# Three weight loads of an expert stage wait for the rows of group 1 instead of the candidates' rows

## The chip, the core and the metric

The kernel runs on one core of a Trainium2 chip. The metric is the device time of one execution in microseconds, as the median of several runs; the profile shows one execution of the same program, and its span is a little shorter than that execution's time. The engines are named as in the profile: PE (matmul), DVE (vector), ACT (scalar), POOL, and SP, which here only issues transfers.

## What is computed

Attention in chunks of 64 keys gives a matrix x of 4608 rows and 512 columns. A gate picks one of 8 experts for each row; each expert keeps at most 80 rows, those with the highest gate weight, and runs a two-layer network on them. All other rows of the output are zero.

```python
expert_idx = np.argmax(x @ w_gate, axis=1)
...
for e in range(E):
    tok_idx = np.where(expert_idx == e)[0]
    ...                                    # at most `capacity` of them, by gate weight
    h = np.maximum(x[tok_idx] @ w1[e], 0.0)
    out[tok_idx] = gate_w[tok_idx, None] * (h @ w2[e])
```

Here w1 of one expert is 512 x 1024 and w2 is 1024 x 512, both in 32-bit floats, 2 MB each.

## The kernel before

Attention, gate and choice of rows fill the first 132 us or so; x is written to a scratch tensor `xs` in DRAM on the way. The expert stage follows, and only it matters here.

**Rows and groups.** Each of the 8 experts has 96 slots, three quarters of 32. Six groups r = 0 to 5 of 128 slots, four quarters each, are worked off one after the other. Quarter g of group r belongs to expert (4r + g) // 3, so group 0 needs experts 0 and 1, group 1 experts 1 and 2, group 2 experts 2 and 3, group 3 experts 4 and 5, group 4 experts 5 and 6, group 5 experts 6 and 7. The rows of group 0 come another way: two gathers `xc[0]` and `xc[1]` (lines 876 to 878) fetch the candidates' rows of experts 0 and 1 while the ranking still runs, and a matmul (line 920) sorts them into `xT0`. The rows of groups 1 to 5 are gathered by POOL with an indirect transfer each (`gather`, line 181; `rows`, line 170) into the tiles `xg[r]`, 128 rows of 2 KB, once their row numbers `gic` are there (line 151).

**Order on PE.** For each group: first layer, first half of its columns (`layer1(r, 0)`, line 207); transposes of the group before (`hpose`, line 225); transposes of the next group's rows (`xpose`, line 193); first layer, second half; second layer of the group before (`layer2`, line 241). Group 1's transposes stand in the middle of `layer1(0, 1)` (lines 203 and 204): 48 of group 0's 64 first-layer matmuls lie ahead of them.

**Order on SP.** One queue issues all large transfers, in the order of the program. The weights of experts 0 and 1 and w1 of expert 2 (line 968) are loaded before the expert stage. `ahead(r, ...)` (line 960) issues what list r of `LATER` names: pair (e, 0) is w1 of expert e, (e, 1) its w2, (e, 2) a clear, which writes 1 MB of zeros to block e of the output.

```python
LATER = [[(2, 1), (3, 0), (3, 1)], [(4, 0), (5, 0), (0, 2)], [(4, 1), (5, 1), (1, 2)], [(6, 0), (6, 1), (2, 2), (7, 0)], [(7, 1), (3, 2), (4, 2), (5, 2), (6, 2), (7, 2), (8, 2)], [], [], []]
```

List 0 is issued before group 0's first layer, list r + 1 after group r. Where `part` (line 950) is given a column `after`, DVE first copies that column into the weight tile (line 957), and the load, which overwrites it, has to wait for the copy; this holds the load back until `after` is there. Only the three loads of list 0 have such a copy: in the kernel before, the w2 of expert 2 is tied to `xc[0]`, both loads of expert 3 to `xc[1]`. The weight tiles of experts 5, 6 and 7 reuse buffers of earlier experts and so also wait for PE.

**The end.** POOL scatters each group's result into the output (line 260), and no scatter may start before all nine clears have landed.

Of the kernel before, what the change touches and what calls it, by code (L numbers as in the profile page):

```python
# [54 lines left out]
def attention_moe(ctx: ExitStack, tc: tile.TileContext, qk, vv, wg, w1, w2, cap, cst, out):  # L55
# [50 lines left out]
    weights = {}  # L106
# [34 lines left out]
    def place(pool, pp, pt, sel, cb, tag, r0=0, r1=NR):  # L141

        pl = (pp([P, r1 - r0, 5]) if pt is None else
              pp.tile([P, r1 - r0, 5], F32, name=f"pl{tag}{r0}", tag=pt))
        for g in range(4 * r0, 4 * r1):
            o = 32 * (g % 4)
            nc.tensor.matmul(pl[o:o + 32, g // 4 - r0, :], lhsT=sel(*divmod(g, 3)),
                             rhs=cb[:, :, g // 3], start=True, stop=True, tile_position=(0, o))
        gi = pool.tile([P, r1 - r0], I32, name=f"gi{tag}{r0}", tag=f"gi{r0}")
        with nc.allow_low_precision(reason="row numbers are whole and far below 2^24"):  # L150
            nc.vector.tensor_reduce(gi, pl[:, :, 0:2], axis=AX.X, op=ALU.add)
        return pl, gi

    def targets(pool, places, tag):

        gate = pool.tile([P, NR], F32, name=f"gate{tag}", tag="gate")
        row = pool.tile([P, NR], F32, name=f"row{tag}", tag="row")
        r0 = 0
        for pl, gi in places:
            cols = slice(r0, r0 + gi.shape[1])  # L160
            r0 = cols.stop
            nc.vector.tensor_reduce(gate[:, cols], pl[:, :, 2:5], axis=AX.X, op=ALU.add)
            nc.vector.tensor_reduce(row[:, cols], pl[:, :, 0:2], axis=AX.X, op=ALU.add)
        sv = pool.tile([P, NR], F32, name=f"sv{tag}", tag="sv")
        nc.vector.scalar_tensor_tensor(
            sv, gate, 0.0, ct[:, C_OOB:C_OOB + NR], op0=ALU.is_equal, op1=ALU.mult)
        nc.vector.tensor_tensor(sv, sv, row, op=ALU.add)
        return gate, sv
# [5 lines left out]
            in_offset=bass.IndirectOffsetOnAxis(ap=at, axis=0),  # L174
            bounds_check=NT * 512 - 1, oob_is_err=False)

    def experts(pool, pp, gi, si, gate, getw, tag, extra=None, xc=None, xT0=None):
        groups = [[(4 * r + g) // 3 for g in range(4)] for r in range(NR)]
        xg, xT, hs, hT = {}, {}, {}, {}

# [5 lines left out]
        def xpose(r):  # L186
            t = pool.tile([P, 4, P], F32, name=f"xt{tag}{r}", tag="xt")
            n = 4 if r else 2
            for b0 in range(0, 4, n):
                pm = pp.tile([P, n, P], F32, name=f"xp{tag}{r}_{b0}", tag="hp" if b0 else "xp",  # L190
                             bufs=2 if b0 else 1)
                for b in range(n):
                    nc.tensor.transpose(pm[:, b, :], xg[r][:, P * (b0 + b):P * (b0 + b + 1)],  # L193
                                        ident)
                nc.scalar.copy(t[:, b0:b0 + n], pm)
            xT[r] = t
# [69 lines left out]
        for r in range(1, NR) if extra else range(2):  # L266
            gather(r)
        if extra:
            extra(0, xc)
            xT[0] = xT0  # L270
            y0 = pp.tile([P, DM], F32, name=f"y{tag}0", tag="y", bufs=1)
        else:
            xpose(0)
# [17 lines left out]
    with ExitStack() as actx:  # L291
# [371 lines left out]
        def clear(n, eng=nc.sync):  # L663

            r0 = 512 * n
            eng.dma_start(
                out[r0:r0 + 4 * P].rearrange("(p c) d -> p c d", p=P),
                zero[:, None, :].to_broadcast([P, 4, DM]))
# [16 lines left out]
        with tc.manual_schedule():  # L685
# [190 lines left out]
            xc = [mp.tile([P, DM], F32, name=f"xc{e}") for e in range(2)]  # L876
# [39 lines left out]
            xT0 = mp.tile([P, 4, P], F32, name="xT0")  # L916
# [18 lines left out]
            pl, gi = place(mp, bank, None, sel_part, cb, "c")  # L935
            gate, sv = targets(mp, [(pl, gi)], "c")
            nc.vector.tensor_tensor(sv, sv, slot_oob, op=ALU.add)
            si = mp.tile([P, NR], I32, name="si")
# [5 lines left out]
    with tc.manual_schedule():  # L944
        with ExitStack() as ectx:
            ep = ectx.enter_context(tc.tile_pool(name="exp", bufs=2, reuse_waits="tile"))
            pp = ectx.enter_context(tc.tile_pool(name="pexp", bufs=2, space=PSUM,
                                                 reuse_waits="tile"))

            def part(e, l, after=None):  # L950

                w = weights.setdefault(e, [None, None])
                pool = wp if e in (5, 6) else wp2
                a, src, n = ((4, w1, FF), (8, w2, DM))[l]
                w[l] = pool.tile([P, a, n], F32, name=f"w{l + 1}_{e}", tag=f"w{l + 1}")
                if after is not None:
                    nc.vector.tensor_copy(w[l][:, 0, 0:1], after)
                nc.sync.dma_start(w[l], src[e].rearrange("(c p) f -> p c f", p=P))

            def ahead(r, xg):  # L960

                for e, l in LATER[r]:
                    if l < 2:
                        part(e, l, xg[e - 2][:, 0:1] if r == 0 else None)
                    else:
                        clear(e, nc.sync)

            part(2, 0)
            experts(ep, pp, lambda r: gi[:, r:r + 1], si, gate, weights.get, "c", ahead, xc, xT0)


    with tc.If(nc.values_load(flag_i[0:1, 0:1], min_val=0, max_val=1) > 0):  # L972
        with ExitStack() as gctx:
# [59 lines left out]
            with tc.For_i(0, nc.values_load(nr[0:1, 0:1], min_val=0, max_val=48), 1):  # L1033
                with ExitStack() as lctx:
                    xp = lctx.enter_context(tc.tile_pool(name="gx", bufs=1))
                    si = xp.tile([P, NR], I32, name="gsi")
                    with ExitStack() as pctx:
                        lp = pctx.enter_context(tc.tile_pool(name="gpc2", bufs=1, space=PSUM))
                        cand, cb = compact(xp, lp, ptok, "g")
                        pl = place(xp, lp, "pl", lambda e, j: id_b[:, 32 * j:32 * j + 32], cb, "g")  # L1040
                        gate, sv = targets(xp, [pl], "g")
                        nc.vector.tensor_copy(si, sv)
                        nc.vector.tensor_scalar(ptok, ptok, -float(SL), None, op0=ALU.add)
                    with ExitStack() as pctx:
                        lp = pctx.enter_context(tc.tile_pool(name="gpe", bufs=2, space=PSUM))
                        ep = pctx.enter_context(tc.tile_pool(name="gex", bufs=1))
                        gw = {}

                        def getw2(e):
                            if e not in gw:  # L1050
                                gw[e] = load_w(wp2, e, "g")
                            return gw[e]
                        experts(ep, lp, lambda r: pl[1][:, r:r + 1], si, gate, getw2, "g")
# [67 lines left out]
```

## Time and profile before

| | |
|---|---|
| median of 3 runs | 238.54 us (238.28 to 240.3) |
| the profiled execution | 238.45 us |
| its span | 236.6 us |
| PE busy | 219.5 us, 93% of the span |
| DMA queue of SP | 81.31 MB |
| gathers and scatters (POOL's queue) | 3.15 MB |
| weight loads of 2 MB each | 12, median 16.8 us from issue to landing |

A busy PE is not a PE at its peak. "Landing" counts from the start of the issue, and behind other transfers in the queue it is mostly waiting. PEclk is the granted clock of PE, 1.00 for 2.4 GHz and 0.50 for 1.2 GHz.

### The profile page before, as it was taken

What the parts mean: (1) busy time and instruction counts of PE and PEld (TensorE: products, weight loads), DVE (VectorE), ACT (ScalarE), POOL (GpSimd) and SP (SyncE); (2) the same over time, 40 slices, a digit from 0 to 9 for tenths busy, and PEclk for the clock granted to TensorE, in tenths of its full rate; (3) what the DMA queues carried; (4) which work ended last, traced back from release to release, by engine and by line L of the source; (5) the groups of instructions that cost most, each with busy time, mean ns of one, the idle gap of its engine ahead of it and who ended that gap; (6) DMA issues with size and microseconds to landing.
All of it is one profiled execution on the core that took longest, in us unless ns stands there. A gap on an engine that the chain in (4) does not pass through costs nothing.

```text
span 236.6 us, 7355 instructions
## 1 busy us (share of the span) xinstructions
PE 219.5 (93%) x3195; PEld 141.0 (60%) x3195; DVE 115.7 (49%) x249; ACT 67.0 (28%) x119; POOL 57.9 (24%) x158
## 2 busy tenths in 40 slices
PE   8789999999999999989889959999999999999960
PEld 5689889898988888878668412424334343233210
DVE  7858677878787868787686501202111112111110
ACT  2214433545454545454632110202002011010000
POOL 9300401222222222228785440000000000000641
PEclk9999999999999999999999997999999999999997
DMA  6999999999999999999996499999999999999231
GB/s 253 398 413 377 395 406 409 408 408 409 408 410 400 390 399 343 339 372 407 404 414 229 125 386 407 389 409 414 399 408 417 409 415 397 404 405 352 84 115 40
DMA packets 34822, 84.99 MB, mean 359 GB/s; under 512 B 3040, under 2 KB 3168, under 8 KB 34784
## 3 DMA queue, kind: packets, MB, share of 16 engines
q1 hardware_dynamic: 33744, 81.31, 89.2%
q0 software_dynamic: 1040, 3.15, 3.6%
q8 instruction: 27, 0.44, 0.7%
q14 instruction: 11, 0.09, 0.1%
HBM read 64.27 MB, written 20.45 MB: 358 GB/s over the span
## 4 chain that ended last, share of the span: by engine, by line
PE 81%; DMA 8%; DVE 3%; issue 3%; SPq 1%; POOL 1%; ACT 1%; POOLq 0%; ACTq 0%
PE yc L241 17%; PE hc L207 16%; PE o L428 15%; PE s L371 13%; PE px L400 5%; PE pt L400 4%; DMA qb<-in_qk 3%; PE small L480 3%; DMA xgc<-xs,gic 3%; PE hpc L225 3%; DMA xc<-xs,gi_c 1%; PE xpc L193 1%; PE two L862 1%; PE small L491 1%; PE small L603 1%
## 5 line engine op out<-in xcount | busy, mean ns | idle before, releaser
L241 PE MATMUL yc<-w,htc 128*32 128x512 f32 x384 | 42.3, 592 | 0.0
L207 PE MATMUL hc<-w,xtc 128*32 128x512 f32 x320 | 37.2, 606 | 0.0
L428 PE MATMUL o<-vb,pT 128*64 128x130 f32 x576 | 36.1, 276 | 0.7 <-ACT pT L409 0.7
L371 PE MATMUL s<-qb 128*64 128x128 f32 x512 | 31.5, 276 | 2.1 <-DMA qb<-in_qk 1.7
L428 PEld LDWEIGHTS o<-vb,pT 128*64 128x64 f32 x576 | 31.6, 135 | 1.9 <-ACT pT L409 0.8
L371 PEld LDWEIGHTS s<-qb 128*64 128x64 f32 x512 | 27.7, 137 | 4.3 <-issue 2.8
L241 PEld LDWEIGHTS yc<-w,htc 128*32 128x32 f32 x384 | 12.4, 110 | 28.3 <-issue 28.3
L382 DVE TENSOR_REDUCE mx<-s 128x16 f32<-128x1024 f32 x18 | 22.0, 1225 | 13.5 <-PE s L371 12.8
L409 ACT ACTIVATE pT<-pt 128x1024 f32<-128x1024 f32 x18 | 18.3, 1024 | 30.3 <-PE pt L400 30.3
L260 POOL DMA_INDIRECT out<-ysc,to x6 | 5.9, 990 | 85.3 <-SPq L972 81.3
L207 PEld LDWEIGHTS hc<-w,xtc 128*32 128x32 f32 x320 | 10.2, 113 | 23.1 <-issue 23.1
L471 ACT COPY xT<-px 128x1024 f32<-128x1024 f32 x17 | 17.1, 1007 | 22.0 <-PE px L400 22.0
L443 DVE TENSOR_TENSOR x<-o,rc 128x1024 f32<-128x1024 f32 (+1 forms) x20 | 22.4, 1118 | 0.7
L387 DVE TENSOR_TENSOR sm<-s,mx 128x1024 f32<-128x1024 f32 x18 | 22.1, 1227 | 0.6
L212 ACT ACTIVATE hsc<-hc 128x512 f32<-128x512 f32 x6 | 3.6, 597 | 63.5 <-PE hc L207 63.5
L246 DVE TENSOR_SCALAR ysc<-yc,gatec 128x512 f32<-128x512 f32 x6 | 4.5, 751 | 33.5 <-PE yc L241 33.5
L214 DVE TENSOR_SCALAR hsc<-hc 128x512 f32<-128x512 f32 x6 | 4.2, 692 | 26.7 <-PE hc L207 26.7
L229 DVE COPY htc<-hpc 128x512 f32<-128x512 f32 x6 | 4.2, 692 | 22.9 <-PE hpc L225 22.9
L581 ACT ACTIVATE lv<-io_b,bo 128x256 bf16<-128x256 bf16 x29 | 12.5, 499 | 0.8 <-DVE bo L561 0.6
L400 PE MATMUL pt<-ct,sm 64*128 64x64 f32 x288 | 12.6, 228 | 0.0
L400 PE MATMUL px<-ct,x 64*128 64x64 f32 x272 | 12.2, 229 | 0.0
L400 PEld LDWEIGHTS pt<-ct,sm 64*128 64x128 f32 x288 | 10.3, 139 | 2.9 <-issue 2.8
(147 smaller groups left out, 226.6 us busy)
## 6 DMA issues: line engine op xcount, KB each, us to landing
w<-in_w SPq DMA_DIRECT2D x12, 2048.0 KB, 16.8
qb<-in_qk SPq DMA_DIRECT2D x32, 512.0 KB, 7.9
vb<-in_vv SPq DMA_DIRECT2D x36, 260.0 KB, 7.0
out<-zero SPq DMA_DIRECT2D x9, 1024.0 KB, 16.0
xs<-x SPq DMA_DIRECT2D x16, 512.0 KB, 7.6
w<-in_w SPq DMA_DIRECT2D x16, 512.0 KB, 8.0
w<-in_qk SPq DMA_DIRECT2D x4, 512.0 KB, 5.3
xs<-x SPq DMA_DIRECT2D x4, 256.0 KB, 8.3
```

The costliest lines, as they stand in the source:

```text
L207: nc.tensor.matmul(h[o:o + 32, :], lhsT=xT[r][:, b, o:o + 32], rhs=getw(groups[r][g])[0][:, b, 512 * f:512 * f + 512], start=(b == 0), sto ...
L225: nc.tensor.transpose(pm[:, j, :], hs[r][:, P * c:P * c + P], ident)
L241: nc.tensor.matmul(y[o:o + 32, :], lhsT=hT[r][c // 4][:, c % 4, o:o + 32], rhs=getw(groups[r][g])[1][:, c, :], start=(c == 0), stop=(c == ...
L371: nc.tensor.matmul(ps[64 * u:64 * u + 64, t, P * pr:P * pr + P].rearrange("p (h k) -> p h k", h=2), lhsT=t8[:, 1, pr, u, :], rhs=t8[:, 0:3 ...
L382: nc.vector.tensor_reduce(d['mx'], d['s8'], axis=AX.X, op=ALU.max)
L387: nc.vector.tensor_tensor(d['sm'].rearrange("p c k h -> p h c k"), d['s8'], d['mx'][:, :, :, None].to_broadcast([P, 2, 8, 64]), op=ALU.sub ...
L400: nc.tensor.transpose(at[:, 64 * c:64 * c + 64], src(c)[rows], ident[rows, rows])
L409: nc.scalar.activation(d['pT'], pt, AF.Exp, scale=0.125)
L428: nc.tensor.matmul(po[64 * u:64 * u + 64, o:o + 130].rearrange("p (h x) -> p h x", h=2), lhsT=d['pT'][:, u, c:c + 64], rhs=v[:, :, pr, u, ...
L443: nc.vector.tensor_tensor(TT[T][:, r:r + nt, :].rearrange("p r (k h e) -> p (r k) h e", k=4, h=2), pov[..., 0:64], rc[:, :, :, None].to_br ...
L471: nc.scalar.copy(XT[n].rearrange("p c u j -> p u c j"), pm.rearrange("p u (c j) -> p u c j", j=64))
L581: nc.scalar.activation(lv, io_b, AF.Sign, bias=bo[:, rt:rt + 1], scale=-1.0)
```

## The change

The column that the three loads of list 0 wait for is now `xg[1]`, the rows of group 1, for all three. Since `xg` is what `ahead` gets anyway after each group, the parameter `xc` of `experts` goes.

```diff
-    def experts(pool, pp, gi, si, gate, getw, tag, extra=None, xc=None, xT0=None):
+    def experts(pool, pp, gi, si, gate, getw, tag, extra=None, xT0=None):
...
         if extra:
-            extra(0, xc)
+            extra(0, xg)
             xT[0] = xT0
...
                 for e, l in LATER[r]:
                     if l < 2:
-                        part(e, l, xg[e - 2][:, 0:1] if r == 0 else None)
+                        part(e, l, xg[1][:, 0:1] if r == 0 else None)
...
-            experts(ep, pp, lambda r: gi[:, r:r + 1], si, gate, weights.get, "c", ahead, xc, xT0)
+            experts(ep, pp, lambda r: gi[:, r:r + 1], si, gate, weights.get, "c", ahead, xT0)
```

## Rows read from the trace of the kernel before

**Rows 1.** The page's head: the span.
```profile
span 236.6 us, 7355 instructions
```

**Rows 2.** The chain that ended last: start us, us, what.
```profile
127.49 3.33 DMA xc<-xs,gi_c
...
132.78 7.52 DMA xgc<-xs,gic
...
141.00 6.98 PE hc L207 x48
...
149.01 0.44 PE xpc L193 x4
149.45 3.57 PE hc L207 x32
...
159.89 3.43 PE hc L207 x32
...
190.55 3.43 PE hc L207 x32
...
205.88 3.43 PE hc L207 x32
```

**Rows 3.** Stretches: length, busy of PE, PEld, DVE, ACT, POOL; clock, DMA share, GB/s.
```profile
128.00:129.00 1.00, 1.00 (x12) 0.88 (x10) 0.93 (x6) 0.00 (x0) 0.49 (x1) 1.00 0.75 258
142.00:143.00 1.00, 1.00 (x10) 0.22 (x4) 0.00 (x0) 0.00 (x0) 0.00 (x0) 0.50 1.03 397
...
131.80:136.00 4.20, 4.00 (x62) 1.47 (x65) 1.59 (x11) 0.65 (x2) 2.61 (x3) 1.00 0.58 167
136.00:140.00 4.00, 1.82 (x20) 0.32 (x12) 0.00 (x0) 0.60 (x1) 2.57 (x4) 1.00 1.02 385
140.00:145.00 5.00, 4.65 (x28) 1.54 (x32) 0.69 (x1) 0.58 (x1) 0.00 (x0) 0.68 1.04 399
145.00:217.00 72.00, 72.00 (x660) 24.93 (x652) 9.93 (x14) 8.19 (x14) 0.00 (x0) 1.00 1.04 406
```

**Rows 4.** Timeline (start, duration us; idle before); and line 172's five gathers (duration ns).
```profile
131.67 0.56 DVE L957 COPY w<-xc 128x1 f32<-128x1 f32 x3
...
131.89 16.81 SPq L958 DMA_DIRECT2D w<-in_w  x5
...
140.35 0.66 PE L193 MATMUL xpc<-ct,xgc 128*128 128x128 f32 x4 [2.52 <-DMA xgc<-xs,gic]
...
L172 POOL DMA_INDIRECT xgc<-xs,gic x5: 994/998/999, 132.8 to 138.0; - x5
```

**Rows 5.** Issue (ns, start us) and landing (us): w1 of experts 3, 6, 7, last clear.
```profile
L958 SPq DMA_DIRECT2D w<-in_w x1: 524/524/524, 132.4 to 132.4; - x1
...
DMA to landing us min/median/max: 17.3/17.3/17.3
...
L958 SPq DMA_DIRECT2D w<-in_w x1: 2551/2551/2551, 170.0 to 170.0; - x1
...
DMA to landing us min/median/max: 16.0/16.0/16.0
...
L958 SPq DMA_DIRECT2D w<-in_w x1: 2589/2589/2589, 182.6 to 182.6; - x1
...
DMA to landing us min/median/max: 16.2/16.2/16.2
...
L666 SPq DMA_DIRECT2D out<-zero x1: 2603/2603/2603, 206.4 to 206.4; - x1
...
DMA to landing us min/median/max: 13.1/13.1/13.1
```

**Rows 6.** Timeline of POOL at the end: first, fifth and sixth scatter.
```profile
220.48 1.04 POOL L260 DMA_INDIRECT out<-ysc,to  x1 [81.29 <-SPq L972]
...
226.36 0.98 POOL L260 DMA_INDIRECT out<-ysc,to  x1 [0.28 <-issue]
...
230.39 0.98 POOL L260 DMA_INDIRECT out<-ysc,to  x1 [2.86 <-DVE ysc L246]
```

## The prediction

> **What bounds the kernel now.** I read the chain that ended last first. From 141 us on its links are matmuls of the expert stage without a gap, up to the last scatter; ahead of them stands one long transfer, the gather of group 1's rows, 7.52 us from issue to landing, while a gather of the same size on the same line, `xc[1]`, took 3.33 [rows 2]. Group 1's transposes start at 140.35 after 2.52 us in which PE had nothing to do [rows 4], so PE ran dry at 137.83; soon after it works at a granted clock of 0.50, which is 1.2 GHz, as the stretch from 142 to 143 shows [rows 3]. So the chain holds a stall and its echo.
>
> Second I read the stretches, because the chain shows only who ended last. The DMA engines carry 406 GB/s from 145 to 217 us at a share of 1.04 [rows 3]: the transfers are as full as PE. Over that time one queue, in one order, moves weights and clears, and whatever delays its start by D delays every landing by D. The reader should see two lines that run side by side to the end: PE, and SP's stream of transfers.
>
> Third I read where the second line touches the first. Two points matter. The w1 of expert 6 is issued at 170.05 and lands 16.0 us later, at 186.05 [rows 5]; group 4's first layer wants it at 190.55 [rows 2], 4.5 us later. And the last clear, issued at 206.4, lands at 219.5 [rows 5]; the first scatter starts at 220.48 after a wait that the row puts on SP, not on PE [rows 6]. Scatters one to five start at 220.48 to 226.36, 1.47 us apart, so the sixth could start at 227.83; it starts at 230.39, when its data are there [rows 6]. POOL thus has 2.56 us to spare against PE.
>
> **What the change does.** No instruction is added or taken away. Three copies on DVE, 0.56 us together, and the three loads behind them wait for another tile [rows 4]. A copy now follows gather 1, so it moves past the row numbers (line 151) on DVE's queue; behind it on DVE nothing is needed before group 0's ReLU, whose matmuls are not finished at that time, so the wait costs nothing on DVE. If that cover were gone, what waits is the ReLU of group 0 and with it `hpose(0)`. On SP it is different: the w2 of expert 2 is at the head of the queue, and all other loads and clears stand behind it. That delay is the price.
>
> *Gain on PE.* In the kernel before, gather 1 shares the engines with the loads, which SP issues at 131.89, 0.9 us ahead of it [rows 2, 4]. Now it runs alone. I take 3.33 us from `xc[1]` [rows 2]: landing at 132.78 + 3.33 = 136.11, ahead of 137.83. The bounds are 3.33 and the 7.52 of the crowded one; I take the lower, since gather 1 would have as little beside it as `xc[1]` had. The stall of 2.52 goes. With it goes the slow clock: the transposes took 0.66 where the next ones took 0.44, and 48 matmuls took 6.98 where 32 take 3.57, so 48 take 5.36 [rows 2, 4]. That is 0.22 + 1.62. Gain: 2.52 + 0.22 + 1.62 = 4.4 us, at group 1.
>
> *Loss on the stream.* A landing at 140.30 let PE start at 140.35 [rows 2, 4], and from the first copy's start to the first load's issue it is 131.89 - 131.67 = 0.22 us [rows 4]. So SP issues at 136.11 + 0.05 + 0.22 = 136.4, 4.5 us later than before. The stream doesn't lose all of that, since the gathers, 5 x 0.262 = 1.31 MB, used to run amid the loads and now run partly ahead of them. I count bytes up to 140.5, which is 4.5 us past the end of the loads' slow start at 136. Before (1 GB/s is 1 KB per us): 4.2 x 167 + 4 x 385 + 0.5 x 399 = 2440 KB [rows 3]. After: the same slow start of the loads, 4.2 x 167 = 700 KB, now from 136.3 to 140.5, and gather 1, 262 KB, ahead of it. What the other gathers move during the slow start is the open price. Least: nothing, 960 KB in all, D = (2440 - 960) / 406 = 3.6 us. Most: their own pace, one per 1.3 us [rows 4], 3.2 of them, 850 KB, 1810 in all, D = 1.55. Between them I take what the engines have free: the slow start leaves 1.04 - 0.58 of a share for 4.2 us, 1.93, and gathers alone move 258 KB per 0.75 of a share [rows 3], so 660 KB, 1620 in all, D = 820 / 406 = 2.0 us. Should gather 1 take some 0.4 us longer, D grows by about 0.3.
>
> The rows speak of a trade that isn't even: from 131.8 to 136 the share is 0.58 [rows 3], so a load that comes late leaves engines idle. The Trainium skill, "DMA: Bandwidth & Descriptors", section "Issuing engines are not separate DMA queues", says that transfers of all engines run on the same 16 DMA engines and interleave; by that alone the stream would lose what gather 1 gains, and the sum would be 236.5 instead of 237.9.
>
> *The sum.* With D = 2.0, the w1 of expert 6 lands at 188.05, while PE, 4.4 us ahead, wants it at 186.15. A new wait of 1.9 us arises, and PE's lead shrinks to 2.5. The w1 of expert 3 (landing at 132.4 + 17.3 = 149.7, wanted at 159.89) and that of expert 7 (198.8, wanted at 205.88) have 10.2 and 7.1 us [rows 2, 5], less PE's lead of 4.4 and 2.5, against a delay of 2.0: no wait. If PE's clock falls again after the new wait, as it did after the 2.52 us, that costs up to 1.84 more, and the lead is 0.66. The clears end 2.0 later, too: the first scatter at 222.5, the sixth ready at 227.83 + 2.0 = 229.8, against 230.39 before. So the last scatter moves by max(-2.5, 2.0 - 2.56) = -0.56 us, and with the slower clock by the same -0.56. Nearly half of the 4.4 us goes into the wait for expert 6's weights, and most of the rest into the wait for the clears, which set the end. On the profiled execution, 238.45 us (its span of 236.6 [rows 1] and 1.85 around it), this gives 237.9. That execution is 0.1 below the median shown, which I don't correct for.
>
> **The rivals.**
>
> *The stream loses next to nothing.* If engines made up at once for the late start, the loads would lose only gather 1's bytes, 0.262 MB at 406 GB/s, D = 0.65: the scatters move by 0.65 - 2.56 = -1.9, to 236.5. The rule of the Trainium skill quoted above comes to the same. Even at D = 0 POOL's spare of 2.56 bounds the gain: 235.9. Against it: the slow start itself, a share of 0.58 for 4.2 us [rows 3], for which I see no reason to vanish.
>
> *The scatters start without the clears.* Then PE's lead of 2.5 us alone counts: 235.95, faster by just over 1%. Against it: the row of the first scatter waits on SP's side, and it starts 0.98 us after the last clear's landing [rows 5, 6].
>
> *The gather is no faster alone* (the other side). If the 7.52 us are POOL's five issues in a row (132.8 to 138.0 [rows 4]) and not the loads beside them, gather 1 lands at 140.3 as before, PE keeps stall and slow clock, and SP issues at 140.57, 8.7 us late. Bytes up to 144.7: before 4.2 x 167 + 4 x 385 + 4.7 x 399 = 4115 KB; after, 1310 of gathers and 700 of the slow start; D = 2105 / 406 = 5.2. The scatters move by 5.2 - 2.56 = +2.6: 241.1, slower by 1.1%. It decides from D = 4.95 on. Against it: `xc[1]`, too, was one of a pair of gathers, and took 3.33.
>
> *The loads get no credit for the gathers* (D = 3.6 to 4.5). The end moves by +1.0 to +1.9: 239.5 to 240.4, within 1%. With D = 3.6 and a second slow clock, PE loses 3.5 + 1.84 of its 4.4 and comes to +0.9, no later than POOL.
>
> **How the numbers follow.** A measurement of this kernel can tell about 1% from no change, 2.4 us. The forecast with D from 1.2 to 3.6, 237.1 to 239.5, gets 0.65; no credit, to 240.4, gets 0.15; the stream that loses next to nothing 0.07, a quarter of it at 236.05 or less; scatters without the clears 0.03; the slow gather 0.1, all of it slower by over 1%. That is faster 0.05, same 0.85, slower 0.1. The range takes in the forecast, nearly all of the case without credit and the upper end of the faster ones: 236.9 to 240.3.
>
> **What would show it.** Right: gather 1 lands 3.3 to 3.8 us after its issue; no idle time of PE ahead of group 1's transposes; clock 1.00 through 145 us; SP's loads issued from about 136.4; a new idle time of PE of 1.5 to 2.5 us, put on a weight load, ahead of group 4's first layer; the last clear landing 2 us later; six scatters back to back, 1.47 us apart, none waiting for its data. Wrong: a landing of gather 1 after 138; the last clear within 0.5 us of its old place (then the stream lost nothing); a wait for weights at another group; the sixth scatter still waiting for data, which would put PE, not the clears, last.

## The result: slower by 0.7%

| | before | after |
|---|---|---|
| median, 20 runs each | 238.63 us | 240.14 us |
| profiled execution | 238.45 us | 239.59 us |
| its span | 236.6 us | 237.8 us |

The ratio after to before is 1.0071, with a 95% interval of 1.0042 to 1.010. The time lies in the range that the prediction gave, but on the other side of before: a gain of 0.55 us was forecast (238.45 to 237.9), and a loss of 1.1 (profiled executions) to 1.7 us (ratio) was measured.

Four views of the changed kernel answer to rows of before. First the timeline at the start of the expert stage (start, duration, engine and line, and in brackets the idle time before, with what ended it), which answers to [rows 4]:

```profile
132.83 1.00 POOL L172 DMA_INDIRECT xgc<-xs,gic  x1 [4.37 <-DVE rowc L163]
136.28 0.43 DVE L957 COPY w<-xgc 128x1 f32<-128x1 f32 x3 [2.47 <-DMA xgc<-xs,gic]
136.49 1.00 SPq L958 DMA_DIRECT2D w<-in_w  x2
...
137.80 0.66 PE L193 MATMUL xpc<-ct,xgc 128*128 128x128 f32 x4
```

Gather 1 is there when DVE's copies start, at 136.28; SP issues its first load at 136.49, and PE goes into group 1's transposes with no idle time at all. Then the stretches (columns as in [rows 3]):

```profile
131.80:136.30 4.50, 4.29 (x63) 1.56 (x66) 1.33 (x9) 0.65 (x2) 2.86 (x3) 1.00 0.31 80
136.30:140.50 4.20, 4.20 (x40) 1.35 (x36) 0.34 (x3) 1.18 (x2) 2.33 (x4) 1.00 0.80 211
140.50:145.00 4.50, 4.50 (x44) 2.07 (x36) 0.82 (x2) 1.14 (x2) 0.00 (x0) 1.00 1.00 374
...
190.00:191.00 1.00, 1.00 (x8) 0.20 (x4) 0.00 (x0) 0.00 (x0) 0.00 (x0) 0.50 1.04 406
```

The clock is 1.00 at group 1 now, and 0.50 at 190. Up to 145 the engines have moved 360 + 886 + 1683 = 2930 KB since 131.8; in the kernel before it was 700 + 1540 + 1995 = 4235 KB [rows 3]. Third, issue and landing of gather 1, of gather 4, of expert 6's w1 and of the last clear, which answer to [rows 5] (ns of the issue, its start in us; below, us to landing):

```profile
L172 POOL DMA_INDIRECT xgc<-xs,gic x1: 997/997/997, 132.8 to 132.8; - x1
...
DMA to landing us min/median/max: 3.4/3.4/3.4
...
L172 POOL DMA_INDIRECT xgc<-xs,gic x1: 999/999/999, 136.7 to 136.7; - x1
...
DMA to landing us min/median/max: 8.2/8.2/8.2
...
L958 SPq DMA_DIRECT2D w<-in_w x1: 2511/2511/2511, 173.4 to 173.4; - x1
...
DMA to landing us min/median/max: 16.2/16.2/16.2
...
L666 SPq DMA_DIRECT2D out<-zero x1: 2602/2602/2602, 209.9 to 209.9; - x1
...
DMA to landing us min/median/max: 13.0/13.0/13.0
```

Expert 6's w1 lands at 189.6 instead of 186.05, the last clear at 222.9 instead of 219.5. Fourth, the timeline ahead of group 4 and at the end, which answers to [rows 6]:

```profile
186.12 1.03 PE L207 MATMUL hc<-w,xtc 128*32 128x512 f32 x4
...
189.64 1.92 PE L207 MATMUL hc<-w,xtc 128*32 128x512 f32 x5 [2.49 <-DMA w<-in_w]
...
224.04 1.04 POOL L260 DMA_INDIRECT out<-ysc,to  x1 [84.80 <-DVE ysc L246]
...
229.64 0.75 DVE L246 TENSOR_SCALAR ysc<-yc,gatec 128x512 f32<-128x512 f32 x1 [6.12 <-PE yc L241]
229.92 0.98 POOL L260 DMA_INDIRECT out<-ysc,to  x1 [0.28 <-POOL to L259]
231.37 0.98 POOL L260 DMA_INDIRECT out<-ysc,to  x1 [0.28 <-POOL to L259]
```

The kernel before in the same view, at group 4 and at the last result:

```profile
190.37 2.33 PE L207 MATMUL hc<-w,xtc 128*32 128x512 f32 x20
...
228.87 0.75 DVE L246 TENSOR_SCALAR ysc<-yc,gatec 128x512 f32<-128x512 f32 x1 [6.12 <-PE yc L241]
```

Counted from the issue of gather 1 (132.78 before, 132.83 now), PE reaches group 4 4.3 us ahead of before, at 53.29 instead of 57.59. It does four matmuls of expert 5, stands still for 2.49 us until expert 6's weights are there, and then works at the slow clock. This spends more than the lead: the last result starts at 96.81, 0.72 us later than the 96.09 of before. The scatters run back to back, and the sixth has no wait for its data any more, but only just: before, it started 1.52 us behind the start of that result, which now makes 231.16, and its turn comes at 231.37. (The bracket at 224.04 names DVE, but DVE's result of that time was ready at 223.52 and belongs to the fifth scatter; the clear landed at 222.9. A wait for several things is put down to the one that came last.)

Executions differ by up to 2.3 us in when the expert stage begins (gather 1 is issued at 132.61 in e2, at 134.93 in e1), so below I count from the issue of gather 1: the first scatter comes 87.70 us after it in the kernel before (220.48 - 132.78) and 91.21 in the changed one, the last 97.61 and 98.54. The first figure less 87.70 is D, the delay of SP's stream, in the runs that leave no clear out and move none.

### The profile page after: what moved, and what is told of

Its sections match the earlier page's. It is cut to its first block, busy times and chain, and to the rows that moved or that the text cites. A ratio compares the mean times of both kernels' runs of the same rounds, so it can differ in the third digit from the quotient of the medians.

```text
span 237.8 us, 7354 instructions
## 1 busy us (share of the span) xinstructions
PE 219.9 (92%) x3195; PEld 140.6 (59%) x3195; DVE 115.6 (49%) x249; ACT 67.0 (28%) x119; POOL 58.0 (24%) x158
## 4 chain that ended last, share of the span: by engine, by line
PE 73%; DMA 12%; SPq 7%; DVE 3%; issue 1%; POOL 1%; ACT 1%; POOLq 0%; ACTq 0%
PE o L428 15%; PE hc L207 14%; PE s L371 13%; PE yc L241 12%; DMA w<-in_w 7%; PE px L400 5%; PE pt L400 4%; SPq L666 4%; DMA qb<-in_qk 3%; PE small L480 3%; PE hpc L225 2%; DMA xc<-xs,gi_c 2%; SPq L958 1%; PE pwarm L920 1%; PE two L862 1%
## 5 line engine op out<-in xcount | busy, mean ns | idle before, releaser
L207 PE MATMUL hc<-w,xtc 128*32 128x512 f32 x320 | 38.8, 614 | 2.5 <-DMA w<-in_w 2.5
```

Of the source, the lines that this page charges most:

```text
L207: nc.tensor.matmul(h[o:o + 32, :], lhsT=xT[r][:, b, o:o + 32], rhs=getw(groups[r][g])[0][:, b, 512 * f:512 * f + 512], start=(b == 0), sto ...
```

## The experiments

Three theories. **Clears**: D holds back the last clear, and with it the scatters. **Wait**: D holds back expert 6's w1, and that wait with its slow clock makes PE late. And on D itself, **trade**: while the loads start, a gather's bytes are paid for by the loads; against it **idle** (the whole delay is lost) and **disturbance** (gathers make the start of the loads longer). The middle columns of the table are from one profiled execution each, the last one from all runs.

| run | first load after gather 1's issue | gather 1 lands after | first scatter after | last scatter after | time to before (interval) |
|---|---|---|---|---|---|
| before | -0.89 | 7.5 | 87.70 | 97.61 | 1 |
| changed | 3.66 | 3.4 | 91.21 | 98.54 | 1.0071 (1.0042 to 1.010) |
| e1 | 3.68 | 3.4 | 91.19 | 98.52 | 1.0042 (1.0004 to 1.008) |
| e2 | 3.52 | 3.3 | 85.61 | 96.28 | 0.9999 (0.9959 to 1.004) |
| e3 | 3.68 | 3.4 | 86.10 | 93.46 | 0.9883 (0.983 to 0.9937) |
| e4 | 1.22 | 3.4 | 89.43 | 96.78 | 0.9979 (0.994 to 1.0017) |
| e5 | 9.10 | 3.5 | 94.39 | 101.73 | 1.0176 (1.0106 to 1.0245) |
| e6 | 0.24 | 7.6 | 88.93 | 97.56 | 0.9972 (0.9939 to 1.0005) |
| e7 | 1.22 | 7.4 | 89.22 | 96.55 | 1.0000 (0.9965 to 1.0034) |
| e8 | -0.83 | 7.8 | 82.86 | 97.88 | 1.0028 (0.9987 to 1.0069) |
| e9 | 3.79 | 3.5 | 90.83 | 98.17 | 1.0049 (1.0015 to 1.0083) |
| e10 | 1.22 | 3.7 | 89.44 | 96.78 | 1.0018 (0.9984 to 1.0051) |
| e11 | -0.83 | 7.5 | 87.67 | 97.50 | 0.9987 (0.9945 to 1.003) |
| e12 | 1.22 | 3.8 | 86.88 | 93.39 | 0.9887 (0.9835 to 0.9939) |

### e1: two clears later, expert 6 sooner

```diff
- [(4, 0), (5, 0), (0, 2)], [(4, 1), (5, 1), (1, 2)], ... [(7, 1), (3, 2), ...
+ [(4, 0), (5, 0)], [(4, 1), (5, 1)], ... [(7, 1), (0, 2), (1, 2), (3, 2), ...
```

> The changed kernel, with the clears of blocks 0 and 1 moved from between the weight loads to the front of the six last clears. Nothing is left out; the w1 of expert 6 stands 2 MB further ahead in SP's queue and lands 5.2 us sooner, near 184.4, before PE wants it at 186.1. Clear theory (the last scatter is late because SP's stream, and with it the last clear, ends 3.5 us later): the wait and the slow clock ahead of group 4 go, PE ends 4.4 us ahead of the kernel before, the scatters still run back to back from 224.0 to 231.4, and the time stays that of the changed kernel, 0.6 to 0.8% slower than before. Wait theory (the wait for expert 6 and the slow clock behind it made it slower): the time falls by 4 us against the changed kernel, 1.0 to 1.2% faster than before.

Timeline of e1, and its stretches around group 4, which starts at 188.2 (PE's busy time stands behind the length, the clock is the seventh figure):

```profile
134.93 1.00 POOL L172 DMA_INDIRECT xgc<-xs,gic  x1 [4.18 <-DVE rowc L163]
...
226.12 1.04 POOL L260 DMA_INDIRECT out<-ysc,to  x1 [84.78 <-SPq L972]
...
228.96 0.75 DVE L246 TENSOR_SCALAR ysc<-yc,gatec 128x512 f32<-128x512 f32 x1 [8.35 <-DMA out<-ysc,to]
...
233.45 0.98 POOL L260 DMA_INDIRECT out<-ysc,to  x1 [0.28 <-POOL to L259]
...
180.00:190.00 10.00, 10.00 (x100) 3.05 (x96) 1.44 (x2) 0.00 (x0) 0.00 (x0) 1.00 1.04 413
190.00:200.00 10.00, 10.00 (x96) 3.72 (x92) 1.39 (x2) 1.77 (x3) 0.00 (x0) 1.00 1.04 409
```

In e1 PE has no wait at group 4 and no slow clock, and the scatters come within 0.02 us of where they were: 91.19 and 98.52 after gather 1's issue. All of PE's lead is lost at the end; the last result even waits on DVE for a buffer that the first scatter has to give back. The time is 0.4% over before, a little under the 0.6 to 0.8 expected, which the interval takes in. The wait theory alone falls.

### e2 and e3: two clears left out, without and with e1's order

```diff
- [(7, 1), (3, 2), (4, 2), (5, 2), (6, 2), (7, 2), (8, 2)]
+ [(7, 1), (3, 2), (4, 2), (5, 2), (6, 2)]
```

> The changed kernel without the clears of blocks 7 and 8, so the rows of these blocks that no expert keeps are not written with zeros. The last clear lands 5.2 us sooner, near 217.8, and POOL has its first five scatters out by 226. Clear theory in its plain form (the clears alone set the end): 3.5 us less than the changed kernel or more. Both together, as the trace of the changed kernel has it (the last result is ready for its scatter at 231.2, the sixth scatter's turn comes at 231.4): the end moves by only 0.2 us, since PE with its wait and its slow clock at group 4 is as late; 0.5 to 0.7% slower than before.

> Both edits of the two runs before on the changed kernel: the clears of blocks 0 and 1 late, those of blocks 7 and 8 left out. If PE's wait and the clears are two equal bounds with one cause, the delay of SP's stream, only here does the 4.4 us gained at group 1 come through: PE ends near 224.4, the sixth scatter's turn comes at 226.2, and the time is 4 to 5 us less than the changed kernel's, 1.1 to 1.7% faster than before. If something else holds the end, less than 2 us.

The timeline of e2 at group 4 and at the last scatter, and its clock behind the wait (the seventh figure of the stretch, counted from its length):

```profile
188.85 3.63 PE L207 MATMUL hc<-w,xtc 128*32 128x512 f32 x28 [1.93 <-DMA w<-in_w]
...
228.89 0.98 POOL L260 DMA_INDIRECT out<-ysc,to  x1 [3.59 <-DVE ysc L246]
...
190.00:192.00 2.00, 2.00 (x20) 0.49 (x12) 0.00 (x0) 0.00 (x0) 0.00 (x0) 1.00 1.05 410
```

With the clears out of the way PE sets the end. I had expected 0.2 us, but in this execution the wait was 1.93 us and the clock stayed at 1.00, so the last scatter came 2.3 us sooner than in the changed kernel. This execution is the fastest of e2's twelve (236.65 us, with a median of 238.95); over all runs e2 is level with before, where 0.5 to 0.7% over it was expected. Without the wait alone (e1) the end stays, without two clears alone it moves: the clears are thus the tighter of the two bounds, and PE's wait the next one. That its size depends on whether the clock falls is read from one execution of each kernel. Only with both gone (e3) does the gain of group 1 come through, 1.2% under before; last scatter of e3:

```profile
133.27 1.00 POOL L172 DMA_INDIRECT xgc<-xs,gic  x1 [4.16 <-DVE rowc L163]
...
226.73 0.98 POOL L260 DMA_INDIRECT out<-ysc,to  x1 [0.28 <-POOL to L259]
```

That is 93.46 us after gather 1's issue, 4.15 under before, nearly the 4.3 us of lead that PE had at group 4.

### e8: two clears left out of the kernel before

> The kernel before without the clears of blocks 7 and 8, so the rows of these blocks that no expert keeps are not written with zeros; the last clear lands 5.2 us sooner. In the kernel before the sixth scatter waits 2.56 us beyond its turn for its data, so PE sets the end there and a shorter stream is worth nothing: within 0.4% of before. If the clears set the end in the kernel before, too, it is over 1% faster.

The same two clears are left out as in e2. The first scatter comes 4.8 us sooner, the last not at all (97.88 against 97.61), and the time is level: in the kernel before, the clears had room, as read in [rows 6].

### e5: loads behind all five gathers

```diff
- part(e, l, xg[1][:, 0:1] if r == 0 else None)
+ part(e, l, xg[5][:, 0:1] if r == 0 else None)
```

> The changed kernel with the three loads tied to the rows of group 5, the last gather (issued 5.2 us behind gather 1), so that all five gathers, 1.31 MB, are through before SP issues a load: near 9.9 us after gather 1's issue plus 0.7, 9.9 us later than in the kernel before. Trade theory (in the slow start of the loads a gather's bytes and a load's bytes cost each other in full, and ahead of it a gather is free): the stream is late by 9.9 us less the 1.31 MB at 406 GB/s, 3.2 us, so 6.6 us; first scatter 94.3 us after gather 1's issue (87.7 before, 91.2 in the changed kernel); the time 1.5 to 1.9% over before. Idle theory (the stream loses the whole delay, whatever runs ahead of it): 9.9 us late, 2.8 to 3.2% over before.

Timeline, and the stretch of the loads' start in e5:

```profile
134.55 0.99 POOL L172 DMA_INDIRECT xgc<-xs,gic  x1 [4.22 <-DVE rowc L163]
...
143.65 13.75 SPq L958 DMA_DIRECT2D w<-in_w  x5
...
228.94 1.04 POOL L260 DMA_INDIRECT out<-ysc,to  x1 [87.98 <-DVE ysc L246]
...
143.55:147.75 4.20, 4.20 (x42) 1.57 (x35) 0.94 (x4) 0.52 (x1) 0.00 (x0) 1.00 0.59 171
```

D is 94.39 - 87.70 = 6.7 us after a delay of 10.0: the five gathers' 3.2 us are credited in full, as the trade theory had it (6.6), and the idle theory falls. The stretch shows more: with no gather beside them the loads start at 171 GB/s for 4.2 us, as they did in the kernel before with 167. The slow start thus belongs to the loads: it is there without any gather.

### e9 and e10: later gathers out of the loads' start

```diff
+ # row numbers of gathers 4, 5 (e9), 3 to 5 (e10), behind layer1(0, 1)
+ nc.vector.tensor_copy(gl[:, j:j + 1], gi(j))
+ gather(j)
```

> The changed kernel with gathers 4 and 5 issued later: their row numbers are copied by DVE behind group 0's second ReLU, so POOL issues them from about 141.5 instead of at 136.7 and 138.0, out of the slow start of the loads (136.5 to 140.7), and they are not wanted before 175. It measures the price that the prediction got wrong. Trade theory (a gather's bytes in the slow start come out of the loads' bytes, nothing else is lost): the two gathers are paid for later instead, the first scatter stays 91.0 to 91.4 us after gather 1's issue (91.2 in the changed kernel, 87.7 before) and the time within 0.3% of the changed kernel's. Disturbance theory (gathers in the slow start also make it longer): the slow start is that of the kernel before again, the stream is late by 4.6 us less three gathers at 0.65 us, 2.6 us; the first scatter comes 90.3 us after gather 1's issue and the time is 0.3 to 0.5% less than the changed kernel's.

> The kernel with the loads tied to si, and gathers 3 to 5 issued only behind group 0's second ReLU, near 141.5, so that only gather 1 and gather 2 are in flight while the loads start. Trade theory: first scatter 89.4 us after gather 1's issue as with si, time as with si, 0 to 0.5% less than before. Disturbance theory: the stream is late by 2.1 less 0.65 us, 1.45; first scatter at 89.1, and the sixth at its turn 0.3 us sooner, 0.2 to 0.6% less than before. Either way gather 1 is in time, and PE has no idle time ahead of group 1's transposes.

e9's first scatter comes at 90.83, e10's at 89.44 (e4, the same tie with all gathers together: 89.43). So of the disturbance theory's 0.9 us in e9 some 0.4 show in that one execution, and in e10 nothing. The 0.4 are no more than executions with the same start of the loads differ by: the third of the tied loads lands 25.6 us after gather 1's issue in e9, 25.6 in e1 and e3, 26.0 in the changed kernel. The trade theory is enough for both. In time neither differs from its sibling beyond the intervals.

### e4, e6, e11: when a load holds a gather

```diff
- part(e, l, xg[1][:, 0:1] if r == 0 else None)
+ part(e, l, si[:, 0:1] if r == 0 else None)                        # e4
+ part(e, l, gate[:, 0:1] if r == 0 else None)                      # e6
+ part(e, l, (xg[1] if e == 3 else xc[0])[:, 0:1] if r == 0 else None)   # e11
```

> The changed kernel with the three loads tied to si (line 940), which DVE has at 133.8, instead of to the rows of group 1: SP issues them near 134.1, 2.2 us later than in the kernel before and 2.4 us sooner than in the changed one. Order theory (what holds a gather is a load whose bytes come before the gather's; one already moving is not held): gather 1, whose bytes begin 2.1 us after its issue at 132.8, lands by 137, PE keeps its 4.4 us at group 1, the stream is 1.5 to 2.2 us late instead of 3.5, and the end is 0.4 to 1.0 us sooner than in the kernel before, 0.2 to 0.5% faster. Crowd theory (any load issued before gather 1 has landed holds it): gather 1 lands near 140, the stall and the slow clock at group 1 are back, and the time is that of the kernel before or up to 1 us more.

> The changed kernel with the three loads tied to gate (line 162), which DVE has at 132.6; by the order of DVE's queue the first copy runs near 132.85, and SP issues near 133.05, 0.9 us sooner than with si and 1.2 us later than in the kernel before, 0.3 us after gather 1's issue. Order theory: the loads' first bytes come 1.3 us after their issue, near 134.4, gather 1's own near 134.9, so the loads are first again, gather 1 lands near 140 and PE stands still ahead of group 1's transposes as in the kernel before; with the stream 0.5 to 1 us late the time is that of before or up to 0.3% more. If instead nothing but the loads' landing matters, gather 1 is in time as with si, the stream is only 0.8 us late and the time is 0.5 to 0.8% less than before.

> One part of the change alone: the two loads of expert 3 wait for the rows of group 1, the w2 of expert 2 for the candidates' rows as in the kernel before. SP issues one load of 2 MB at 131.9 and the rest after gather 1. Order theory: its bytes come before gather 1's and hold it, so the gather lands 5 to 7.5 us after its issue, PE stands still at group 1 for 0.5 to 2.5 us; the stream has 2 MB to carry (5.2 us at 406 GB/s) until the next load is there, so it is late by 0 to 2 us; time within 0.5% of before. If one load alone doesn't hold a gather: landing within 4 us, PE keeps its 4.4 us, stream less than 1 us late, and the time 0.5 to 1% less than before.

Timelines of the three, one after the other:

```profile
132.75 1.00 POOL L172 DMA_INDIRECT xgc<-xs,gic  x1 [4.25 <-DVE rowc L163]
133.97 13.04 SPq L958 DMA_DIRECT2D w<-in_w  x4
...
137.71 0.65 PE L193 MATMUL xpc<-ct,xgc 128*128 128x128 f32 x4
```

```profile
133.32 1.00 POOL L172 DMA_INDIRECT xgc<-xs,gic  x1 [4.33 <-DVE rowc L163]
133.56 13.74 SPq L958 DMA_DIRECT2D w<-in_w  x4
...
140.99 1.12 PE L193 MATMUL xpc<-ct,xgc 128*128 128x128 f32 x4 [2.63 <-DMA xgc<-xs,gic]
```

```profile
133.86 0.37 SPq L958 DMA_DIRECT2D w<-in_w  x1
134.69 1.00 POOL L172 DMA_INDIRECT xgc<-xs,gic  x1 [4.22 <-DVE rowc L163]
...
222.36 1.04 POOL L260 DMA_INDIRECT out<-ysc,to  x1 [81.26 <-SPq L972]
```

A load issued 0.24 us behind gather 1 (e6) holds it as much as one issued 0.89 ahead: 7.6 us to landing. Issued 1.22 us behind (e4), it doesn't hold it: 3.4 us. In between, other gathers of these runs are held a little: gather 3, issued 0.91 to 1.08 us ahead of the first load in the changed kernel, e1, e2 and e3, takes 4.2 to 4.6 us. The order theory fits this (a load's first bytes come 1.0 us behind its issue in e5 and in the kernel before, a gather's 1.7 us in e5 and in the changed kernel; my expectations had 1.3 and 2.1), but no view tells the bytes of the two apart, so it stays inferred. e11 shows that the one load at the head of SP's queue makes the difference: with it tied as before, the stream is as before (87.67), the gather is held (7.5 us), and the time is as before, though two of the three loads wait for the rows of group 1. e4 and e6 come out 0.2 and 0.3% under before, with intervals that take in no change; e4's last scatter, 0.83 us under before, is what D less POOL's spare gives (1.73 - 2.56).

### e7: a clear in the idle time ahead of the loads

```diff
+ nc.vector.tensor_scalar(zero[:, 0:1], xc[0][:, 0:1], 0.0, None, op0=ALU.mult)
+ clear(0, nc.sync)                                 # ahead of e4's loads
```

> The kernel with the loads tied to si, and the clear of block 0 issued ahead of them, where SP's queue stands idle: one element of the zero tile is made from the candidates' rows times zero, so that the clear starts when those are there, near 131.9. Nothing is left out. If a transfer of 1 MB in the idle stretch is free, the rest of the stream is 1 MB shorter: last clear 2.6 us sooner than with si, expert 6's w1 too, no wait at group 4, and the time 0.8 to 1.5% less than before. If the clear's bytes, first in line, hold gather 1 until they are through (near 136 to 137), it lands at 137.5 to 138.5, PE waits up to 0.7 us at group 1 and the time is 0.4 to 1.0% less than before. If they hold it as the loads did in the kernel before (landing at 140), there is no gain against si.

```profile
132.91 0.60 SPq L666 DMA_DIRECT2D out<-zero  x1
...
133.51 7.05 PE L207 MATMUL hc<-w,xT 128*32 128x512 f32 x48 [0.21 <-ACT xT L923]
...
133.83 1.00 POOL L172 DMA_INDIRECT xgc<-xs,gic  x1 [4.16 <-DVE rowc L163]
...
141.24 0.65 PE L193 MATMUL xpc<-ct,xgc 128*128 128x128 f32 x4 [0.68 <-DMA xgc<-xs,gic]
```

No gain: 1.0000 (0.9965 to 1.0034), so of the three cases expected the last one came. The clear, issued 0.92 us ahead of gather 1, held it for 7.4 us (133.83 to 141.24); the first scatter came at 89.22, where e4 had 89.43, though the stream behind the tie is 1 MB shorter. PE had to wait only 0.68 us, because in this execution its clock was 0.50 from 134 to 137 and the 48 matmuls ahead took 7.05 us; with the 5.36 us that they took in the changed kernel the wait would have been 2.4 (an estimate from these rows). e5's execution began in the same way.

### e12: what the runs suggest, together

```diff
+ part(e, l, si[:, 0:1] if r == 0 else None)
+ if n == 14: clear(0)                    # in the attention stage, not in LATER
+ # the six copies to[r] on POOL once behind the gathers, not ahead of each scatter
```

> Three edits on the changed kernel that follow from the runs: the loads tied to si; the clear of block 0 issued inside the attention stage (step 14), where the DMA engines have room from 92 to 96 us; and the six copies of scatter rows on POOL made once behind the gathers, not one ahead of each scatter. Nothing is left out. Clear theory, as the other runs bear it out: the stream behind the tie has 1 MB less, 2.6 us, so it ends 0.9 us sooner than in the kernel before instead of 1.7 later; expert 6's w1 is in time; first scatter 86.8 us after gather 1's issue, the scatters 1.3 instead of 1.47 us apart, last one at 93.4 (97.6 before); the last data ready at 93.2. That is 4.2 us less than before, 1.3 to 1.8% faster. If the clear in the attention stage delays the front part by as much as it saves behind, 0.3 to 0.8%; if something else than clears and expert 6 holds the end, no more than with si alone (0.2%).

```profile
133.04 1.00 POOL L172 DMA_INDIRECT xgc<-xs,gic  x1 [4.27 <-DVE rowc L163]
...
219.92 1.04 POOL L259 DMA_INDIRECT out<-ysc,to  x1 [79.89 <-SPq L977]
...
226.43 0.98 POOL L259 DMA_INDIRECT out<-ysc,to  x1 [0.30 <-issue]
...
92.00:96.00 4.00, 4.00 (x80) 3.67 (x80) 3.65 (x10) 3.16 (x7) 1.68 (x8) 1.00 1.05 408
```

First scatter after 86.88 us, last after 93.39, as forecast, and 0.9887 (0.9835 to 0.9939) of the time before. That is 1.1% faster, less than the 1.3 to 1.8 forecast, part of which the interval takes in; by the two ratios it is 1.8% faster than the changed kernel. The last row is a stretch of the attention stage, full with the clear in it; the kernel before had room there:

```profile
92.00:96.00 4.00, 4.00 (x80) 3.69 (x78) 3.83 (x9) 3.62 (x7) 1.70 (x8) 1.00 0.86 300
```

Which of the three edits gives how much was not run one by one, except the first (e4).

## Why the prediction was wrong, step by step

**Right.** Gather 1 alone lands after 3.4 us (3.33 forecast), SP issues at 136.49 (136.4), PE has no idle time at group 1, the clock there stays at 1.00, and PE reaches group 4 4.3 us sooner (4.4). The lead is spent at the two places named: expert 6's weights, with the slow clock behind the wait, and the clears. Six scatters run back to back, 1.47 us apart, and the sixth has no wait. The spare of 2.56 us of POOL in the kernel before is borne out by e8, whose last scatter does not move, and by e4.

**Wrong: the size of D.** D was put at 2.0 us; it is 3.5 (91.21 - 87.70), next to the "least" end of the bounds, 3.6, where the other gathers move nothing for free while the loads start. The step that failed is the choice between the bounds: "Between them I take what the engines have free", 1.93 us of share at 344 KB per share and us, 660 KB. Up to 140.5 it gave 1620 KB in all; the stretches show 360 + 886 = 1246. A share of 0.58 was taken for room in which others can move. The trace has little such room: from 136.3 to 140.5 loads and gathers together moved 211 GB/s, while loads alone start at 171 (e5) and gathers alone reach 258 [rows 3]. Over 4.2 us the gathers thus added some 170 KB, not 660. The sum also stopped too early: up to 145 the changed kernel is 1305 KB behind, 3.2 us at 406 GB/s; where the last 0.3 us of D are lost is open. By these sums gathers 2 and 3, already under way, took their bytes out of the loads' start (inferred, not measured by itself), and gathers 4 and 5 were held themselves, 8.2 and 8.0 us to landing.

**Why that turned the sign.** The end moved by max(PE, D - 2.56), as the sum had it. With D = 2.0 the second term is -0.56, with 3.5 it is +0.95; the last scatter moved by 98.54 - 97.61 = +0.93. PE's term, put at -2.5 or, with the slow clock, -0.66, came to +0.72, for the same reason: expert 6's weights came 1.5 us later than forecast, too. The wait there is shorter than the sum gives for D = 3.5 (2.49 instead of 3.4), because PE first does its four matmuls of expert 5, 1.03 us, which the prediction left out. Beyond the last scatter, the span's end lies 6.43 us behind the last scatter instead of 6.21, which I didn't follow up. What came lies at the lower edge of the rival "no credit" (D from 3.6 on, 239.5 and more), which had a chance of 0.15: D just under it, the profiled execution, 239.59, just in it. So the time is in the range because the range took that rival in, not because the sum was right. With hindsight the rival should have had more, since the row on which the choice could rest, gather 1 held for 7.5 us beside loads that were just starting, stood in the profile and spoke against room.

**The Trainium skill's rule** that transfers interleave on the same 16 engines ("DMA: Bandwidth & Descriptors", "Issuing engines are not separate DMA queues") is borne out as far as the sum of bytes goes: in e5 what the gathers moved ahead of the loads, 3.2 us, is credited in full. It was the even trade (D = 0.65) that didn't come, because the loads' slow start moved with them and its idle share was lost.

## What to carry to other kernels

Where a queue of transfers runs full to the end of a kernel, ask first what the change does to the time at which that stream starts; all that stands at its end, a clear that gates scatters here, moves with it, and a stall removed earlier only turns up there. Free share of the DMA engines is not room for someone else until a row shows two transfers using it side by side. Here a gather got through ahead of a burst of loads that were issued 1.22 us behind it, for half the price of waiting until it had landed (D of 1.7 us in e4 instead of 3.5).

## What the runs showed of the hardware

- A burst of 2 MB loads on an SP queue that has run empty moves little in its first 4.2 us: 162 to 176 GB/s in the kernel before, e5, e6, e8 and e11, and 207 to 243, gathers included, in the changed kernel, e1 to e4, e9, e10 and e12, where a gather issued 1.2 us or more ahead had not landed yet. Later it is 406.
- A gather of 256 KB took 3.3 to 3.8 us from issue to landing where it was issued 1.18 us or more ahead of the first transfer on SP's queue, 4.2 to 4.6 at 0.91 to 1.08 us ahead, and 6.5 to 9.1 at 0.24 us ahead or anywhere behind it.
- PE's granted clock fell to 0.50 (1.2 GHz) behind waits of 2.48 to 3.94 us (the kernel before, the changed one, e5, e6, e8, e11) and stayed at 1.00 behind waits of 1.93 (e2) and 1.86 us (e9). Waits are not all of it: in e5 and e7 it also fell at the start of group 0, where the wait just before had been 0.2 us.
